# Plain fp32 scores for the first head pair alone, idle matmuls at the start, loads held back until the first q has landed, and a longer time for loads in the plan

## The chip, the cores and the metric

The kernel runs on one core of one Trainium2 chip. The metric is the device time of one execution in microseconds; the kernel before was run three times and its median stands. One execution was also profiled, and all rows below are from that one. The engines are PE (TensorE), ACT (ScalarE), DVE (VectorE), POOL (GpSimd) and SP, which issues the transfers (DMA).

## The reference

Attention with rotary positions over 8 batches, 8 heads, 576 positions and 64 columns a head, and then a gated MLP over each batch:

```python
    q_rot, k_rot = (rotate(q), rotate(k))
    scores = scale * np.matmul(q_rot, k_rot.transpose(0, 1, 3, 2))
    scores = scores - np.max(scores, axis=-1, keepdims=True)
    attn = np.exp(scores)
    attn = attn / (np.sum(attn, axis=-1, keepdims=True) + 1e-09)
    return np.matmul(attn, v).astype(np.float32)
...
    h = np.maximum(x @ w_in, 0.0)
    u, v = (h[..., :d_ff // 2], h[..., d_ff // 2:])
    v_n = (v - mu) / np.sqrt(var + 1e-06)
    v_s = np.einsum('ts,bsd->btd', w_spatial, v_n) + b_spatial[None, :, None]
    gated = u * v_s
    return (gated @ w_out).astype(np.float32)
```

The MLP has d_model 512 and d_ff 1024; w_spatial is 576 x 576. Inputs are float32 but for w_in and w_out, which are 64-bit floats.

## The kernel before

The work is cut into 32 head pairs (8 batches of four pairs), numbered i, and one MLP for each batch. Every step of the work is an entry made with `op` (or `either`, where two engines may take it): an engine, a planned cost in ns, a priority key, a function that emits the instructions, the tokens it reads and writes, and the buffers it opens. `Program.run` (L137) then plays all entries through a planned clock: whenever an engine is free it takes the ready entry with the smallest key whose buffers are free, and emits it. So the plan fixes the order of each engine's instructions, and on the chip each engine follows its own order and waits by semaphores. A step counts as done at its cost plus a fixed time of its engine (`LATENCY`, L31; 1700 ns for DMA, 200 for PE). A step with `port=True` is not started while the other of DVE and POOL holds such a step. All transfers go out through SP, in the plan's order. Keys run at about 20 a pair.

A pair's scores are nine row tiles of 128 queries: (head, t) for t = 0 to 3 and one mixed tile t = 4 that holds the last 64 queries of both heads. Each tile goes PE (`scores`, L521), DVE maximum (L557), ACT exponent (L559), through two PSUM buffers (`sc`). There are two ways to make a tile. Pairs below `WHOLE` (L53) use `prepare_whole` (L444): q and k are turned and the fp32 product is taken plainly over the 64 columns of a head (`mm_whole`, L538; rows at L546). All others use `prepare`: q and k are turned in two staging buffers (`stage`), ACT rounds each to fp32r (L416, L427), POOL or DVE takes the rest (`lo_q`, `lo_k`), and ten transfers (L438) stack rounded parts and rests over 128 partitions in `qs`, `ks` and `qz`, of which there is one each; `lk` has one buffer too. Its products are fp32r (`mm`, L528; rows at L536). Pairs below `PLAIN` = 4 take the values with plain transposes (L635) and products (L673) in `values_plain`, the others in `values` (L576, L600).

The start is written out in `prepare_whole` for i = 0: k and the tables come in halves, then q; DVE turns k, sums it, and then turns q in two parts, columns 0 to 191 for tile t = 0 and the rest for the others (L469 to L472). `setup` (L289) makes the identity and the fills on POOL. `decode` (L317) turns the 64-bit weights into rounded float32 parts, twelve times, with keys 30 to 132 (`DEC_V`, `DEC_U`, `DEC_O`); `spatial` (L356) and `spatial_tail` do the like for w_spatial. The MLP's products are at L744, L767, L785 and L800.

Of the kernel before, what the change touches and what calls it, by code (L numbers as in the profile page):

```python
# [16 lines left out]
P = 128  # L17
S = 576
# [11 lines left out]
PE, ACT, DVE, POOL, DMA = "pe", "act", "dve", "pool", "dma"  # L30
LATENCY = {PE: 200, ACT: 142, DVE: 118, POOL: 95, DMA: 1700}  # L31
TO_PE = 105
SLOTS = {
    "stage": 2, "lk": 1, "vraw": 2, "vs": 2, "e2": 4, "e1": 2, "eh": 7, "rb": 1, "x32": 1, "xg": 7, "m": 4,
    "small": 3, "nmx": 3, "rt": 2, "sc": 2, "pv": 1, "pm": 3,
# [14 lines left out]

PLAIN = 4

WHOLE = 3  # L53
Q0 = 3 * TW
CHUNKS2 = [
    ([(0, 0), (1, 0), (0, 1), (1, 1), (0, 2), (1, 2)], [(0, P, 0, 0, 384)]),
# [42 lines left out]
class Op:  # L99
    def __init__(self, costs, key, f, new, port):  # L100
        self.costs, self.key, self.f, self.new, self.port = costs, key, f, new, port
        self.eng = None
        self.waits, self.after, self.bufs = 0, [], []


class Program:
# [5 lines left out]
    def op(self, eng, ns, key, f, r=(), w=(), new=(), port=False):  # L112
        return self.either({eng: ns}, key, lambda e: f(), r, w, new, port)
# [23 lines left out]
    def run(self, make):  # L137
# [29 lines left out]
        while events:  # L167
# [23 lines left out]
            for e in LATENCY:  # L191
                if busy[e]:
                    continue
                passed, chosen = [], None
                while ready[e] and not chosen:
                    item = heapq.heappop(ready[e])
                    if item[2].eng:
                        continue
                    other = {DVE: POOL, POOL: DVE}.get(e)
                    if item[2].port and other and held[other]:  # L200
                        passed.append(item)
                    elif place(item[2].new):
                        chosen = item[2]
                    else:
                        passed.append(item)
                for item in passed:
                    heapq.heappush(ready[e], item)
                if chosen:
                    for b in chosen.new:
                        b.tile = make(b)  # L210
                    chosen.eng = e
                    chosen.f(e)
                    left -= 1
                    busy[e], held[e] = True, chosen.port
                    heapq.heappush(events, (now + chosen.costs[e], n, "free", e))
                    heapq.heappush(events, (now + chosen.costs[e] + LATENCY[e], n + 1, "done", chosen))
                    n += 2
        assert not left, "instructions wait for each other"
        return now
# [3 lines left out]
def tile_attention_gated_mlp(  # L223
# [81 lines left out]
    def load(dst, src):  # L305
        nc.sync.dma_start(out=dst, in_=src)  # L306
# [10 lines left out]
    def decode(key, where, at, src):  # L317
# [38 lines left out]

    def spatial(key, j):
        st = Buf("xg", [P, 2, S], F32, f"ws{j}")
        op(DMA, 1700, key - 8, lambda: load(st.tile, w_spT[j * P:(j + 2) * P, :].rearrange("(c p) t -> p c t", p=P)), w=[st], new=[st])
# [21 lines left out]
    def prepare(i):  # L381
# [24 lines left out]
            pair_op(S, key - K_SUM, f, first=eng, r=[(st[j], 1)], w=[(st[j], 0)])  # L406

        for j in range(2):
            op(DMA, 1640, key - K_LOAD, lambda j=j: load(st[j][:, :2 * S], qk[b, hp, j].rearrange("p c n -> p (c n)")), w=[(st[j], 0), (st[j], 1)], new=[st[j]])
        op(DMA, 910, key - K_LOAD + 1, lambda: load(vr.tile, v[b, hp]), w=[vr], new=[vr])  # L410
        for j, eng, part in ROPE0 if b == 0 else ROPE:
            if part is None:
                rope_sum(j, eng)
# [30 lines left out]
    def prepare_whole(i, b, hp, key):  # L444
# [7 lines left out]
        def turn(st, part, cols):  # L452
            return st[:, S * part:S * part + S][:, cols]
# [5 lines left out]
        if i == 0:  # L459
            for part in range(2):  # L460
                cols = slice(S * part, S * part + S)
                op(DMA, 820, -70 + part, lambda part=part, cols=cols: load(k[:, cols], qk[b, hp, 1, :, part]), w=[(k, part)], new=[] if part else [k])
                op(DMA, 820, -70 + part, lambda part=part, cols=cols: load(tabs[:, cols], tab[:, part]), w=[("tabs", part)])
            op(DMA, 1640, -68, lambda: load(q.tile, qk[b, hp, 0].rearrange("p c n -> p (c n)")), w=[q], new=[q])
            op(ACT, 1053, -50, lambda: nc.scalar.activation(tabq, tabs, AF.Copy, scale=0.125), r=[("tabs", 0), ("tabs", 1)], w=["tabq", "tabs"])
            for part in range(2):
                op(DVE, 680, -60, lambda part=part: nc.vector.tensor_tensor(out=turn(k, part, slice(0, S)), in0=turn(k, part, slice(0, S)), in1=turn(tabs, part, slice(0, S)), op=ALU.mult), r=[("tabs", part)], w=[(k, part)], port=True)
            op(DVE, 830, -59, lambda: sum_k(nc.vector), r=[(k, 0), (k, 1)], w=[kf], new=[kf], port=True)
            for n, (c0, c1) in enumerate(((0, Q0), (Q0, S))):  # L469
                cols = slice(c0, c1)  # L470
                op(DVE, dve_ns(2 * (c1 - c0)), -58 + 2 * n, lambda cols=cols: nc.vector.scalar_tensor_tensor(out=c2(q.tile)[:, :, cols], in0=c2(q.tile)[:, :, cols], scalar=0.125, in1=c2(tabs)[:, :, cols], op0=ALU.mult, op1=ALU.mult), r=[q, ("tabs", 0), ("tabs", 1)], w=[(q, n)], port=True)
                op(DVE, dve_ns(c1 - c0), -57 + 2 * n, lambda cols=cols: nc.vector.tensor_tensor(out=turn(q, 0, cols), in0=turn(q, 0, cols), in1=turn(q, 1, cols), op=ALU.add), w=[(q, n)], port=True)  # L472
        else:
            for j, st in enumerate((q, k)):
                t = ("tabq", "tabs")[j]
                op(DMA, 1640, key - K_LOAD, lambda j=j, st=st: load(st.tile, qk[b, hp, j].rearrange("p c n -> p (c n)")), w=[(st, 0), (st, 1)], new=[st])
# [4 lines left out]
        op(DMA, 910, key - K_LOAD + 1, lambda: load(vr.tile, v[b, hp]), w=[vr], new=[vr])  # L481


    def attention(i):
# [361 lines left out]

    pairs = [(b, hp) for b in range(B) for hp in range(NP)]
    prepped, xs, chain = [], [], []
    op(POOL, 800, -26, setup, w=["ident", "bias", ("sums", 0, 0), ("sums", 1, 0), ("qz", 0), ("qz", 1), ("qs", 0, 0), ("qs", 1, 0)])
# [84 lines left out]
```

## Time and profile before

| | us |
|---|---|
| median of 3 runs | 981.48 |
| lowest and highest | 977.74 and 984.55 |
| the profiled execution | 979.22 |
| its span, first to last instruction | 977.4 |

In the rows, times are microseconds from the span's start unless marked ns. A row of the timeline is: start, duration, engine, source line, operation, what it writes and reads, how often, and in brackets the idle time of the engine before it with what ended it. PE is matmul, PEld the loading of its weights, SPq the issue of a transfer. Ends of matmuls are modelled by the profiler.

### The profile page before, as it was taken

Reading aid. Unit: us, or ns where it says so; the run is one execution under the profiler, and the core shown is the slowest. Engines: PE = TensorE matmul, PEld = TensorE weight load, DVE = VectorE, ACT = ScalarE, POOL = GpSimd, SP = SyncE. Lnnn points to the kernel's source line nnn. Section 1 sums busy time; section 2 is a strip of 40 time slices with the busy share of each in tenths; the row PEclk is TensorE's granted clock in tenths of the full one; section 3 lists DMA queues with packets and bytes.
Section 4 is the critical chain, followed back from the end, with each engine's and each line's share of the span. In section 5 each row is a group of like instructions: output and inputs, shape, how many; then the busy total and the mean of one; then the engine's idle time right before and its main releaser. Section 6 shows DMA issues by size and latency. Waiting matters only on the chain.

```text
span 977.4 us, 19421 instructions
## 1 busy us (share of the span) xinstructions
PE 942.1 (96%) x6618; PEld 853.3 (87%) x6618; DVE 672.1 (69%) x1486; ACT 733.9 (75%) x1827; POOL 571.6 (58%) x500
## 2 busy tenths in 40 slices
PE   4999999999999999999999999999999999999998
PEld 2455689998899989999899988999889998999998
DVE  6999898765866677675776658676686756767331
ACT  3778788777987779776897768877798677976452
POOL 5852445556757657774756766666576765672121
PEclk9999999999999999999999999999999999999999
DMA  7761733454344553345444444445524455330101
GB/s 295 221 197 52 209 100 108 130 128 140 99 139 117 153 150 101 111 120 165 120 130 108 118 151 126 118 128 149 139 76 132 126 156 145 98 93 17 62 2 49
DMA packets 54581, 121.56 MB, mean 124 GB/s; under 512 B 12881, under 2 KB 12881, under 8 KB 54482
## 3 DMA queue, kind: packets, MB, share of 16 engines
q1 hardware_dynamic: 54482, 120.32, 43.1%
q8 instruction: 53, 0.87, 0.4%
q14 instruction: 46, 0.38, 0.1%
HBM read 66.03 MB, written 9.58 MB: 77 GB/s over the span
## 4 chain that ended last, share of the span: by engine, by line
PE 59%; ACT 14%; DMA 9%; DVE 8%; POOL 4%; issue 3%; SPq 2%; DVEq 0%; ACTq 0%; POOLq 0%
PE pc L785 12%; PE sc L536 9%; PE pv L600 8%; PE tp L576 8%; PE pd L800 7%; PE pa L744 4%; PE pb L767 4%; ACT e L559 4%; DMA qs<-st 3%; POOL st L401 2%; ACT eh L587 2%; DVE nmx L557 2%; SPq L306 2%; PE sc L546 2%; ACT vv L827 2%
## 5 line engine op out<-in xcount | busy, mean ns | idle before, releaser
L587 ACT ACTIVATE eh<-tp 128x384 fp32r<-128x384 f32 (+1 forms) x504 | 217.5, 433 | 85.6 <-PE tp L576 69.5
L312 DVE TENSOR_TENSOR el<-tp,eh 128x384 fp32r<-128x384 f32 x336 | 185.9, 554 | 105.1 <-ACT eh L587 92.6
L559 ACT ACTIVATE e<-sc,nmx 128x576 f32<-128x576 f32 x288 | 213.0, 741 | 39.1 <-DVE nmx L557 36.7
L557 DVE TENSOR_REDUCE nmx<-sc 128x1 f32<-128x576 f32 x288 | 215.2, 749 | 31.8 <-PE sc L536 23.4
L576 PE MATMUL tp<-ident,e 128*128 128x128 f32 (+1 forms) x1176 | 197.1, 273 | 11.6 <-ACT ob L803 7.7
L576 PEld LDWEIGHTS tp<-ident,e 128*128 128x128 f32 (+1 forms) x1176 | 144.5, 138 | 30.4 <-ACT ob L803 9.1
L401 POOL TENSOR_TENSOR st<-st,tabq 128x576 f32<-128x576 f32 x55 | 77.7, 1427 | 135.9 <-DMA st<-in_qk_dram 131.0
L600 PE MATMUL pv<-eh,vs 128*128 128x384 f32 (+1 forms) x560 | 154.0, 316 | 0.1
L785 PE MATMUL pc<-wsp,vn 128*128 128x288 f32 x768 | 143.3, 304 | 0.8 <-DVE u L843 0.5
L767 PE MATMUL pb<-x,wi 128*128 128x288 f32 x768 | 142.3, 306 | 0.7 <-ACT u L770 0.7
L800 PE MATMUL pd<-g,wo 128*128 128x288 f32 x768 | 140.8, 304 | 0.0
L744 PE MATMUL pa<-wi,x 128*128 128x512 f32 x448 | 133.0, 407 | 0.0
L536 PE MATMUL sc<-ks,qs 128*128 128x288 f32 x580 | 123.2, 302 | 0.0
L785 PEld LDWEIGHTS pc<-wsp,vn 128*128 128x128 f32 x768 | 115.0, 189 | 3.4 <-DVE u L843 0.9
L710 POOL TENSOR_TENSOR x<-x,rb 128x576 f32<-128x576 f32 x31 | 44.3, 1429 | 123.7 <-DVE x L615 93.4
L767 PEld LDWEIGHTS pb<-x,wi 128*128 128x128 f32 x768 | 112.3, 189 | 4.4 <-PE pb L767 1.4
L800 PEld LDWEIGHTS pd<-g,wo 128*128 128x128 f32 x768 | 113.5, 189 | 2.6
L600 PE MATMUL pv<-el,vs 128*64 128x384 f32 (+1 forms) x448 | 113.7, 295 | 0.0
L536 PE MATMUL sc<-lk,qz 128*128 128x288 f32 x522 | 111.9, 295 | 0.0
L600 PEld LDWEIGHTS pv<-eh,vs 128*128 128x128 f32 x560 | 97.7, 188 | 5.8 <-DVE x L615 1.6
L312 DVE TENSOR_TENSOR eh<-tp,eh 64x256 fp32r<-64x256 f32 (+1 forms) x168 | 59.8, 356 | 61.4 <-ACT eh L587 52.3
L536 PEld LDWEIGHTS sc<-ks,qs 128*128 128x128 f32 x580 | 93.1, 189 | 6.3 <-ACT e L559 0.8
(180 smaller groups left out, 1559.2 us busy)
## 6 DMA issues: line engine op xcount, KB each, us to landing
st<-in_qk_dram SPq DMA_DIRECT2D x63, 576.0 KB
ks<-st SPq DMA_DIRECT2D x116, 160.0 KB
qs<-st SPq DMA_DIRECT2D x116, 144.0 KB
vr<-in_v_dram SPq DMA_DIRECT2D x32, 320.0 KB
out_dram<-ob SPq DMA_DIRECT2D x32, 288.0 KB
qz<-st SPq DMA_DIRECT2D x58, 144.0 KB
ws<-in_w_spT_dram SPq DMA_DIRECT2D x2, 576.0 KB
st<-in_qk_dram SPq DMA_DIRECT2D x2, 288.0 KB
```

The lines of the kernel that those rows point to most:

```text
L312: eng.tensor_tensor(out=lo, in0=src, in1=hi.bitcast(F32), op=ALU.subtract)
L401: f = lambda e: e.tensor_tensor(out=st[j][:, cols], in0=st[j][:, cols], in1=(tabs if j else tabq)[:, cols], op=ALU.mult)
L536: nc.tensor.matmul(pt[:, c * 512:c * 512 + HALF], lhsT=lhsT, rhs=rhs[:, k0 + c * HALF:k0 + (c + 1) * HALF], start=(n == 0), stop=(n == len ...
L557: op(DVE, 665, key + K_MAX, lambda: nc.vector.tensor_reduce(out=nmx.tile, in_=tops(), op=ALU.max, axis=AX.XY, negate=True), r=[pt], w=[nmx ...
L559: op(ACT, 730, key + K_EXP, lambda: nc.scalar.activation(e[:, e0:e0 + S].rearrange("p (c n) -> p c n", c=2), tops(), AF.Exp, bias=nmx.tile ...
L576: nc.tensor.transpose(out=tp[:e.shape[1], m * P:m * P + P], in_=e, identity=ident)
L587: nc.scalar.activation(h, p, AF.Copy)
L600: nc.tensor.matmul(pv[0:rows, c1:c2], lhsT=vs[:, kt, h, vp, :], rhs=part[:, c1:c2], start=(kt == 0 and n == 0 and c1 == 0), stop=last)
L744: nc.tensor.matmul(pm.tile, lhsT=lhsT, rhs=win[1, d][:, j, :], start=(d == 0 and n == 0), stop=(d == 3 and n == len(todo) - 1))
L767: nc.tensor.matmul(pm[:, :HALF], lhsT=win[0, d][:, i, f * P:(f + 1) * P], rhs=x[d][:, at:at + HALF], start=(d == 0 and n == 0), stop=(d == ...
L785: nc.tensor.matmul(pm[:, :HALF], lhsT=lhsT, rhs=rhs, start=(t == 0 and n == 0), stop=(t == 4 and n == 1))
L800: nc.tensor.matmul(pm[:, :HALF], lhsT=wout[d,][:, i, m * P:(m + 1) * P], rhs=gs[d][:, at:at + HALF], start=(d == 0 and n == 0), stop=(d == ...
```

## The change

`WHOLE` goes from 3 to 1: pairs 1 and 2 are prepared and scored like pair 3. Twenty matmuls of the identity with itself are entered on PE with keys from 10000 on, so that the plan takes one only where PE has nothing else that is ready; each opens the one `pv` buffer, whose contents nobody reads. The identity is made in a step of its own with key -80, ahead of the fills. A token "first" is written by the load of the first q, and the loads of all other pairs, of v, of w_in and w_out and of two of the three parts of w_spatial read it: none is issued before q has landed. DVE's steps at the start are merged: the second half of k with its sums, and each part of q with its sum. From pair 4 on the loads of q and k count 1500 ns longer in the plan (`LATE`), which emits nothing.

```diff
+LATE = 1500
-WHOLE = 3
+WHOLE = 1
...
-        self.eng = None
+        self.eng, self.late = None, 0
...
-                    heapq.heappush(events, (now + chosen.costs[e] + LATENCY[e], n + 1, "done", chosen))
+                    heapq.heappush(events, (now + chosen.costs[e] + LATENCY[e] + chosen.late, n + 1, "done", chosen))
...
     def setup():
-        make_identity(nc, ident)
...
-        op(DMA, 1500, key - 8, fetch, w=[t0, t1])
+        op(DMA, 1500, key - 8, fetch, r=["first"], w=[t0, t1])
...
         for j in range(2):
-            op(DMA, 1640, key - K_LOAD, lambda j=j: load(...), w=[(st[j], 0), (st[j], 1)], new=[st[j]])
+            o = op(DMA, 1640, key - K_LOAD, lambda j=j: load(...), r=["first"], w=[(st[j], 0), (st[j], 1)], new=[st[j]])
+            o.late = LATE if i >= 4 else 0
...
-            op(DMA, 1640, -68, lambda: load(q.tile, ...), w=[q], new=[q])
+            op(DMA, 1640, -68, lambda: load(q.tile, ...), w=[q, "first"], new=[q])
...
+            def turn_k(part):
+                nc.vector.tensor_tensor(out=turn(k, part, slice(0, S)), in0=turn(k, part, slice(0, S)), in1=turn(tabs, part, slice(0, S)), op=ALU.mult)
+                if part:
+                    sum_k(nc.vector)
+
+            def turn_q(cols):
+                both = c2(q.tile)[:, :, cols]
+                nc.vector.scalar_tensor_tensor(out=both, in0=both, scalar=0.125, in1=c2(tabs)[:, :, cols], op0=ALU.mult, op1=ALU.mult)
+                nc.vector.tensor_tensor(out=turn(q, 0, cols), in0=turn(q, 0, cols), in1=turn(q, 1, cols), op=ALU.add)
+
+            op(DVE, 680, -60, lambda: turn_k(0), r=[("tabs", 0)], w=[(k, 0)], port=True)
+            op(DVE, 1600, -60, lambda: turn_k(1), r=[("tabs", 1)], w=[(k, 0), (k, 1), kf], new=[kf], port=True)
             for n, (c0, c1) in enumerate(((0, Q0), (Q0, S))):
+                op(DVE, dve_ns(2 * (c1 - c0)) + dve_ns(c1 - c0), -58 + 2 * n, lambda c0=c0, c1=c1: turn_q(slice(c0, c1)), r=[q, ("tabs", 0), ("tabs", 1)], w=[(q, n)], port=True)
...
-    op(POOL, 800, -26, setup, w=["ident", "bias", ...])
+    op(POOL, 800, -80, lambda: make_identity(nc, ident), w=["ident"])
+    op(POOL, 800, -26, setup, w=["bias", ...])
+    for n in range(20):
+        idle = Buf("pv", None, None, f"idle{n}")
+        op(PE, 480, 10000 + n, lambda idle=idle: nc.tensor.matmul(idle[:, :P], lhsT=ident, rhs=ident, start=True, stop=True), r=["ident"], w=[idle], new=[idle])
```

## Rows read from the trace of the kernel before

**Rows 1.** The page: busy time by engine, and the granted clock in 40 slices.

```profile
PE 942.1 (96%) x6618; PEld 853.3 (87%) x6618; DVE 672.1 (69%) x1486; ACT 733.9 (75%) x1827; POOL 571.6 (58%) x500
...
PEclk9999999999999999999999999999999999999999
```

**Rows 2.** Stretches: busy us (and count) by engine, granted clock, DMA share, GB/s.

```profile
10.00:20.00 10.00, 7.20 (x22) 4.70 (x23) 6.96 (x11) 3.18 (x8) 7.88 (x5) 1.00 0.69 279
...
20.00:30.00 10.00, 8.39 (x28) 4.41 (x26) 8.67 (x14) 6.29 (x14) 4.30 (x4) 1.00 0.92 330
...
30.00:100.00 70.00, 65.84 (x382) 36.33 (x382) 65.19 (x112) 57.06 (x137) 37.90 (x35) 1.00 0.47 143
...
110.00:190.00 80.00, 77.93 (x542) 68.72 (x541) 66.97 (x146) 64.80 (x163) 38.96 (x31) 1.00 0.46 122
```

**Rows 3.** Timeline of the start, on POOL, DVE and PE.

```profile
1.02 0.29 POOL masks.py:199 TENSOR_SCALAR_AFFINE_SELECT ident<-ident 128x128 f32<-128x128 f32 x1
...
6.59 0.76 DVE L467 TENSOR_TENSOR st<-st,tabs 128x576 f32<-128x576 f32 x1 [1.24 <-DMA tabs<-in_tab_dram]
...
8.30 1.43 DVE L471 SCALAR_TENSOR_TENSOR st<-st,tabs 128x384 f32<-128x384 f32 x2
...
8.77 0.95 DVE L471 SCALAR_TENSOR_TENSOR st<-st,tabs 128x768 f32<-128x768 f32 x1
...
9.64 0.82 DVE L472 TENSOR_TENSOR st<-st 128x192 f32<-128x192 f32 x2
...
10.05 2.30 PE L546 MATMUL sc<-kf,st 64*128 64x288 f32 x8 [10.05 <-DVE st L472]
```

**Rows 4.** L546's matmuls in 10 to 31, then 38 to 76 us: ns min/median/max.

```profile
L546 PE MATMUL sc<-kf,st x40: 684/684/846, 10.0 to 29.0; 64*128 64x288 f32 x32, 64*64 64x288 f32 x8
...
L546 PE MATMUL sc<-kf,st x72: 402/403/507, 38.0 to 75.5; 64*128 64x288 f32 x56, 64*64 64x288 f32 x16
```

**Rows 5.** Timeline of PE: the same forms at different times.

```profile
25.18 0.90 PE L635 MATMUL tp_0a<-ident,e 128*128 128x128 f32 x3
...
27.49 2.19 PE L546 MATMUL sc<-kf,st 64*64 64x288 f32 x8
...
31.73 1.31 PE L546 MATMUL sc<-kf,st 64*128 64x288 f32 x8
...
49.53 0.55 PE L635 MATMUL tp_0a<-ident,e 128*128 128x128 f32 x3
...
50.48 1.19 PE L546 MATMUL sc<-kf,st 64*64 64x288 f32 x8
```

**Rows 6.** The chain of work that ended last: start, us, engine, tile, line.

```profile
38.12 1.17 PE sc L546 x4
...
88.39 0.52 PE sc L536 x4
```

**Rows 7.** Timeline of SPq and PE, pair 3's values and pair 4's stacking.

```profile
95.00 0.48 SPq L306 DMA_DIRECT2D qs<-st  x1
...
96.53 0.55 PE L635 MATMUL tp_1a<-ident,e 128*128 128x128 f32 x3 [0.75 <-ACT et_0b L642]
...
99.15 0.55 PE L635 MATMUL tp_2a<-ident,e 128*128 128x128 f32 x3 [0.65 <-DVE et_1b L644]
...
101.09 0.50 PE L536 MATMUL sc<-ks,qs 128*128 128x288 f32 x2
```

**Rows 8.** Preparing: the page's POOL group, a step of the chain, POOL's timeline.

```profile
L401 POOL TENSOR_TENSOR st<-st,tabq 128x576 f32<-128x576 f32 x55 | 77.7, 1427 | 135.9 <-DMA st<-in_qk_dram 131.0
...
2.12 4.37 DMA tabs<-in_tab_dram
...
29.83 1.44 POOL L456 TENSOR_TENSOR kf<-st 128x576 f32<-128x576 f32 x1 [1.56 <-PE sc L546]
```

**Rows 9.** Waits after 110 us: us in total, times, longest.

```profile
PE tp L576 <- ACT ob L803: 7.7, 6, 1.5
...
POOL st L401 <- DMA st<-in_qk_dram: 131.0, 24, 7.9
```

More of the change, by code (lines that the diff above doesn't have):

```diff
@@ L358, in spatial @@
         st = Buf("xg", [P, 2, S], F32, f"ws{j}")
-        op(DMA, 1700, key - 8, lambda: load(st.tile, w_spT[j * P:(j + 2) * P, :].rearrange("(c p) t -> p c t", p=P)), w=[st], new=[st])
+        op(DMA, 1700, key - 8, lambda: load(st.tile, w_spT[j * P:(j + 2) * P, :].rearrange("(c p) t -> p c t", p=P)), r=["first"], w=[st], new=[st])
         for c in range(2):
@@ L408, in prepare @@
         for j in range(2):
-            op(DMA, 1640, key - K_LOAD, lambda j=j: load(st[j][:, :2 * S], qk[b, hp, j].rearrange("p c n -> p (c n)")), w=[(st[j], 0), (st[j], 1)], new=[st[j]])
-        op(DMA, 910, key - K_LOAD + 1, lambda: load(vr.tile, v[b, hp]), w=[vr], new=[vr])
+            o = op(DMA, 1640, key - K_LOAD, lambda j=j: load(st[j][:, :2 * S], qk[b, hp, j].rearrange("p c n -> p (c n)")), r=["first"], w=[(st[j], 0), (st[j], 1)], new=[st[j]])
+            o.late = LATE if i >= 4 else 0
+        op(DMA, 910, key - K_LOAD + 1, lambda: load(vr.tile, v[b, hp]), r=["first"], w=[vr], new=[vr])
         for j, eng, part in ROPE0 if b == 0 else ROPE:
@@ L463, in prepare_whole @@
                 op(DMA, 820, -70 + part, lambda part=part, cols=cols: load(tabs[:, cols], tab[:, part]), w=[("tabs", part)])
-            op(DMA, 1640, -68, lambda: load(q.tile, qk[b, hp, 0].rearrange("p c n -> p (c n)")), w=[q], new=[q])
+            op(DMA, 1640, -68, lambda: load(q.tile, qk[b, hp, 0].rearrange("p c n -> p (c n)")), w=[q, "first"], new=[q])
             op(ACT, 1053, -50, lambda: nc.scalar.activation(tabq, tabs, AF.Copy, scale=0.125), r=[("tabs", 0), ("tabs", 1)], w=["tabq", "tabs"])
-            for part in range(2):
-                op(DVE, 680, -60, lambda part=part: nc.vector.tensor_tensor(out=turn(k, part, slice(0, S)), in0=turn(k, part, slice(0, S)), in1=turn(tabs, part, slice(0, S)), op=ALU.mult), r=[("tabs", part)], w=[(k, part)], port=True)
@@ L468, in prepare_whole @@
-            op(DVE, 830, -59, lambda: sum_k(nc.vector), r=[(k, 0), (k, 1)], w=[kf], new=[kf], port=True)
+            def turn_k(part):
[6 more added lines that the diff above has]
+                nc.vector.tensor_tensor(out=turn(q, 0, cols), in0=turn(q, 0, cols), in1=turn(q, 1, cols), op=ALU.add)
@@ L469, in prepare_whole @@
+            op(DVE, 680, -60, lambda: turn_k(0), r=[("tabs", 0)], w=[(k, 0)], port=True)
+            op(DVE, 1600, -60, lambda: turn_k(1), r=[("tabs", 1)], w=[(k, 0), (k, 1), kf], new=[kf], port=True)
             for n, (c0, c1) in enumerate(((0, Q0), (Q0, S))):
-                cols = slice(c0, c1)
-                op(DVE, dve_ns(2 * (c1 - c0)), -58 + 2 * n, lambda cols=cols: nc.vector.scalar_tensor_tensor(out=c2(q.tile)[:, :, cols], in0=c2(q.tile)[:, :, cols], scalar=0.125, in1=c2(tabs)[:, :, cols], op0=ALU.mult, op1=ALU.mult), r=[q, ("tabs", 0), ("tabs", 1)], w=[(q, n)], port=True)
@@ L472, in prepare_whole @@
-                op(DVE, dve_ns(c1 - c0), -57 + 2 * n, lambda cols=cols: nc.vector.tensor_tensor(out=turn(q, 0, cols), in0=turn(q, 0, cols), in1=turn(q, 1, cols), op=ALU.add), w=[(q, n)], port=True)
+                op(DVE, dve_ns(2 * (c1 - c0)) + dve_ns(c1 - c0), -58 + 2 * n, lambda c0=c0, c1=c1: turn_q(slice(c0, c1)), r=[q, ("tabs", 0), ("tabs", 1)], w=[(q, n)], port=True)
         else:
@@ L475, in prepare_whole @@
                 t = ("tabq", "tabs")[j]
-                op(DMA, 1640, key - K_LOAD, lambda j=j, st=st: load(st.tile, qk[b, hp, j].rearrange("p c n -> p (c n)")), w=[(st, 0), (st, 1)], new=[st])
+                op(DMA, 1640, key - K_LOAD, lambda j=j, st=st: load(st.tile, qk[b, hp, j].rearrange("p c n -> p (c n)")), r=["first"], w=[(st, 0), (st, 1)], new=[st])
                 for part in range(2):
@@ L480, in prepare_whole @@
             pair_op(S + TW, key - K_SUM, sum_k, pieces=2, r=[(k, 0), (k, 1)], w=[kf], new=[kf])
-        op(DMA, 910, key - K_LOAD + 1, lambda: load(vr.tile, v[b, hp]), w=[vr], new=[vr])
+        op(DMA, 910, key - K_LOAD + 1, lambda: load(vr.tile, v[b, hp]), r=["first"], w=[vr], new=[vr])
     def attention(i):
@@ L848, in tile_attention_gated_mlp @@
     prepped, xs, chain = [], [], []
-    op(POOL, 800, -26, setup, w=["ident", "bias", ("sums", 0, 0), ("sums", 1, 0), ("qz", 0), ("qz", 1), ("qs", 0, 0), ("qs", 1, 0)])
+    op(POOL, 800, -80, lambda: make_identity(nc, ident), w=["ident"])
+    op(POOL, 800, -26, setup, w=["bias", ("sums", 0, 0), ("sums", 1, 0), ("qz", 0), ("qz", 1), ("qs", 0, 0), ("qs", 1, 0)])
+    for n in range(20):
+        idle = Buf("pv", None, None, f"idle{n}")
+        op(PE, 480, 10000 + n, lambda idle=idle: nc.tensor.matmul(idle[:, :P], lhsT=ident, rhs=ident, start=True, stop=True), r=["ident"], w=[idle], new=[idle])
     prepare(0)
```

## Prediction

> **What bounds the kernel now.** I read the page first: TensorE is busy 942 of 977 us [rows 1], so the end moves only if its work shrinks or its gaps do. The stretches come next [rows 2]. From 110 us on TensorE is full (77.9 of 80 us) and no edit there can do more than close the small gaps. Between 10 and 30 us it is busy for 15.6 of 20 us, and in 30 to 100 it has 65.8 of 70 while VectorE has 65.2. So what the change can win lies ahead of 100 us.
>
> The timeline of the start [rows 3] shows TensorE doing nothing for 10.05 us. The last table half lands just before 6.59, VectorE works through k and then q, and the first scores follow the last VectorE instruction. Of that chain the 0.95 us product over the larger part of q (the x1 row at 8.77, columns 192 on, for row tiles 1 to 4) stands ahead of both sums, and the first tile doesn't need it.
>
> The third thing is hidden by the page. The granted clock reads full in every slice [rows 1], but the same fp32 score matmul takes 684 ns at the median in 10 to 31 us and 403 ns in 38 to 76 [rows 4]. The transposes do the same: three take 0.90 us at 25 us and 0.55 at 49 [rows 5]. The durations say that pair 0's scores run at the lower of TensorE's two levels (1.2 GHz against 2.4), though TensorE was busy three quarters of that time. Only the dense work from 30 us on is quick.
>
> **Scores of pairs 1 and 2.** Before, a pair costs one double tile (two heads side by side, 1.31 us at 31.73), six single tiles of 1.17 and the mixed tile t=4 of 1.19 [rows 5, 6]: 1.31 + 7.02 + 1.19 = 9.5 us. Split into rounded parts, as pair 3 already is, a tile takes 0.52 us [rows 6]; t=4 has six matmuls for four, so 0.78 as an estimate: 8 x 0.52 + 0.78 = 4.9. That is 4.6 us a pair, **9.1 us** for two, on the engine that sets the end.
>
> What it adds beside the path: for each pair two roundings on ScalarE, two subtractions on POOL or VectorE, and ten stacking transfers through SP. POOL has the room (37.9 of 70 us busy in 30 to 100 [rows 2]), so I count the subtractions at nothing; on VectorE the cover is thin. VectorE's 65.2 of 70 us is partly twelve weight decodes that run early because they can. The eight for wi0 and wo have keys above 64, later than much of the scores, and may slide behind 100 us, where VectorE is busy for 67 of 80 us. If the decodes had to finish as early as now, VectorE and not TensorE would set that stretch.
>
> What it adds to the path: qs, ks, qz and lk have one buffer each. Pair 3 could be stacked early because pairs 1 and 2 did not use them; now pair 2 is stacked only behind pair 1's last scores, and pair 3 behind pair 2's. The case before for pair 4 [rows 7]: stacking begins at 95.00 and the first score comes at 101.09, 6.1 us; TensorE fills them with values and loses 0.75 + 0.65 = 1.4 us. Two more such turnovers cost **2.8 us** that way, and 12.2 with nothing to fill them; nothing if values cover all. I take 2.8, because the same values (fourteen groups of transposes a pair at 0.55 and their products) stand ready.
>
> The staging buffer has two slots, one pair. So there is a ring: stacking frees it, the next load goes out, POOL turns and splits, stacking again. By the rows that is 6.1 us + 4.4 (a load's issue to landing, the tables' half) + eight POOL steps of 1.43 [rows 8] = 21.9 us a pair. The pairs now follow each other, from 31.73 to 101.09, at 23.1 us each [rows 5, 7]; less the 4.6 it would be 18.5. If POOL must do it alone, the ring is 3.4 us a pair too slow, 6.8 for two. VectorE's 0.76 us [rows 3] for the same step shortens it, which is why I stay at 2.8.
>
> **The start.** The merged VectorE steps put the first 192 columns of q (product and sum) ahead of the 0.95 us product: **0.9 us** earlier, so the first score near 9.15 (bounds: nothing, if q lands late; 0.9). The gate holds every other load until q has landed, near 8 us, since q is used at 8.30 without a wait. Queued behind that wait on SP are pair 0's and pair 1's loads and all raw weights, in that order. SP had issued them right behind q; now pair 1's data come some 2 us later, as an estimate: the transfers stand still from q's landing until the next issue's data flow, about half of the 4.4 us from an issue to its landing [rows 8]. Pair 1's last k sum ran only at 29.83 and its first score at 31.73 [rows 5, 8], so I count the gate at nothing; without the cover of pair 0's values it costs those 2 us. The five loads of the start meet no others, which can only help.
>
> **The idle matmuls.** The identity is ready at 1.31 [rows 3], and now first on POOL. In the plan they start at 1.0 us and follow each 0.68 us; the first score is planned at about 7.6, so some ten go ahead of it and ten into the gaps between score tiles. A transpose of that size takes 0.30 us at the lower level; an fp32 product has two records, so I estimate 0.6 us, ten in 6 us, done by 7.5, inside the 10.05 us of nothing. Those in the gaps find waits of a microsecond or more (TensorE is busy 15.6 of 20 us), two at a time; I count nothing, at most 3 us for ten at 0.3.
>
> What they bring: at the full level each of the four double tiles needs 1.31 for the 2.30 us of the first [rows 3, 5], and each is followed by maximum, exponent and the next tile's start, so the difference falls on the path: 4 x 0.99 = 4.0. The mixed tile goes from 2.19 to 1.19 (1.0), three groups of transposes from 0.90 to 0.55 (1.05) [rows 5]. Sum **6.0 us** (bounds: 0 if the clock does not hold; 6.0).
>
> The Trainium skill, page "TensorE: Matmul & The Clock Gate", Part 1, says the low clock is the default and activity lifts it; the durations at either side of 31 us agree, and the granted clock of the page does not show it. By that rule alone the gain would be the 6.0 us. The same page, "HAM oscillation", says that an idle stretch of TensorE lowers the clock again; by that the ten early matmuls would be wasted if the stretch up to 9.15 us is idle long enough, and the gain would be 0. No run here shows which.
>
> **Loads counted longer.** This changes only the plan from pair 4 on: turning steps are placed 1.5 us later. POOL waits 131 us for these loads, TensorE's largest wait there is 7.7 us in six places [rows 9]. At best these 7.7 go; at worst a later preparation adds as much. I take 0.
>
> **Sum.** -9.1 - 6.0 - 0.9 + 2.8 = -13.2 us. The profiled execution took 979.2 (span 977.4 and 1.8 around it), so 966.0; the median of the runs is 2.3 above it, 981.5, so **968.3 us**.
>
> **Rivals.**
> *The clock does not hold.* For it: in 10 to 30 us TensorE was busy 15.6 of 20 us and stayed slow, and after the idle matmuls there are some 2 us of nothing. Against it: ten more fill the gaps, and from 80 us on it has gaps of 0.75 us at full speed. Time: 968.3 + 6.0 = 974.3.
> *The ring of staging bounds pairs 1 to 3.* For it: VectorE's 65.2 of 70 us leaves the turning to POOL; then 6.8 for the 2.8 and, since POOL also has the spatial weights to split, a few us more: 973 to 979.
> *Slower.* The same ring, if SP's order is wrong: the stacks of a pair stand behind raw weight loads whose buffers or gate come late, and every pair waits. Pair 1 would begin near 25 us, three pairs follow to pair 4's first score at 101.09: up to 25.4 us each the change gains, from there it loses; at 28.7 us a pair it is 1% slower, 991. Against: nothing in the rows takes 7 us beyond the 21.9.
> *More than forecast.* The longer count takes most of the 7.7: 961.
>
> **How the numbers follow.** Forecast 0.50 (own range 963 to 974), more 0.07, clock 0.18, ring 0.17, slower 0.08. The range leaves out the slower case, half of the best one and the edges: 958 to 982. One per cent, 9.8 us, is about what a measurement here can tell from no change. Below 971.7 lie the best case and most of the forecast, and a little of the two middle ones: 0.55 faster; 0.37 within; 0.08 slower.
>
> **What would show it.** First score near 9.1; L546 medians at 403 ns from the start on (684: the clock rival); fp32r scores of pair 1 near 25 us; pair 4's first score near 88 instead of 101, with TensorE's waits between pairs under 2 us each (if 5 and up, waiting on stacks: the ring); from there on the same busy share to the end. I am wrong if pair 4's first score comes early and the end doesn't, since then VectorE's decodes or the new plan took it back.

## The result, and the profile after

The kernel after takes 969.25 us (median of 4 runs, 967.38 to 971.53), beside 983.01 us for the kernel before in the same comparison (4 runs, 977.74 to 986.14): ratio 0.9862, 95% interval 0.9825 to 0.9899. It is 13.8 us faster. The forecast was 968.3. The time fits; most of the working behind it does not, as the profile shows already. The profiled execution took 971.53 us, its span is 969.8. It lies only 7.7 us below the profiled execution of the kernel before (979.22); the other 6.1 of the 13.8 us stand in the medians and in no trace.

First the page after (busy time; the granted clock in 40 slices), to be read against [rows 1]:

```profile
PE 948.5 (98%) x6654; PEld 863.4 (89%) x6654; DVE 670.6 (69%) x1479; ACT 738.1 (76%) x1837; POOL 580.0 (60%) x507
...
PEclk9999999999999999999999999999999999999999
```

TensorE is busier than before, 948.5 for 942.1 us, in a shorter span: the cheaper scores take work off it, and the idle matmuls put more on (some 16 us by their rows). Then the two long stretches of [rows 2], after (columns as there):

```profile
30.00:100.00 70.00, 64.33 (x415) 40.59 (x413) 65.25 (x112) 57.48 (x142) 43.99 (x39) 1.00 0.75 221
110.00:190.00 80.00, 77.01 (x536) 68.79 (x537) 66.43 (x148) 66.78 (x169) 37.98 (x32) 1.00 0.46 118
```

VectorE has 65.25 of 70 us as before; what grew is POOL (37.90 to 43.99) and the transfers (0.47 to 0.75 of the DMA engines' time). Now the start after, on PE, DVE and SP, the answer to [rows 3]:

```profile
1.37 8.47 PE L862 MATMUL idle<-ident 128*128 128x128 f32 x20 [1.37 <-POOL ident masks.py:199]
10.59 2.30 PE L555 MATMUL sc<-kf,st 64*128 64x288 f32 x8 [0.74 <-DVE st L476]
...
7.56 0.76 DVE L469 TENSOR_TENSOR st<-st,tabs 128x576 f32<-128x576 f32 x1 [2.23 <-DMA tabs<-in_tab_dram]
...
9.59 0.56 DVE L475 SCALAR_TENSOR_TENSOR st<-st,tabs 128x384 f32<-128x384 f32 x1 [0.34 <-DMA st<-in_qk_dram]
...
3.07 1.19 SPq L306 DMA_DIRECT2D wst<-in_w_spT_dram  x2
...
4.83 0.38 SPq L306 DMA_DIRECT2D vr<-in_v_dram  x1
5.26 1.26 SPq L306 DMA_DIRECT2D st<-in_qk_dram  x2
```

Three steps of the prediction fall here. The first score runs at 10.59, not 9.1. It takes the same 2.30 us as before, so the idle matmuls had not lifted the clock by then. And SP issues the small `wst` loads at 3.07, then `vr` and pair 1's `st` at 4.83 and 5.26, long before q is there (VectorE waits for q until 9.59): the token "first" orders the plan, and on the chip nothing waits for it. The line of the plain scores after (ns min/median/max, first and last start) says the same of the clock as the upper row of [rows 4]:

```profile
L555 PE MATMUL sc<-kf,st x32: 684/684/847, 10.6 to 28.9; 64*128 64x288 f32 x32
```

Pair 1's first score comes at 35.77 us and pair 4's at 105.23, where 25 and 88 were forecast and 31.73 and 101.09 stood before [rows 5, 7]:

```profile
35.77 0.51 PE L545 MATMUL sc<-ks,qs 128*128 128x288 f32 x2
...
105.23 0.43 PE L545 MATMUL sc<-ks,qs 128*128 128x288 f32 x2
```

LATE begins at pair 4 and moves that score itself; without LATE (the run late0 below) it comes at 102.33, still behind the 101.09. So not one microsecond was won in the stretch that was to bring all of it. What changed is in TensorE's waits behind 110 us (us in total, times, longest):

```profile
PE tp L585 <- DVE eh L312: 2.1, 2, 1.2
PE sc L545 <- ACT e L568: 1.4, 2, 0.9
PE pc L794 <- DVE el L312: 0.7, 1, 0.7
```

The 7.7 us for ScalarE's evacuation `ob` [rows 9] are gone. To place the gain I cut every kernel's span at two events: the first MLP product `pa` of batch 1 and that of batch 7. Between them lies the same work in all kernels. These are windows of one stretch each, first before, then after:

```profile
230.70:918.10 687.40, 678.00 (x4917) 641.25 (x4917) 473.06 (x1086) 542.63 (x1366) 431.14 (x367) 1.00 0.44 121
```

```profile
229.00:910.50 681.50, 677.60 (x4918) 641.39 (x4917) 473.55 (x1086) 543.37 (x1365) 432.48 (x368) 1.00 0.46 122
```

The six batches take 687.4 us before and 681.5 after. TensorE is busy the same 678 us in both; its idle time fell from 9.4 to 3.9. The start, up to batch 1, brings 1.7 (230.7 to 229.0), the end behind batch 7's first `pa` nothing. The only part of the change that reaches this stretch is LATE, the one that was priced at nothing.

### The profile page after: what moved, and what is told of

The parts are those of the page before. It is cut to its first block, busy times and chain, and to the rows that moved or that the text cites. A ratio compares the mean times of both kernels' runs of the same rounds, so it can differ in the third digit from the quotient of the medians.

```text
span 969.8 us, 19571 instructions
## 1 busy us (share of the span) xinstructions
PE 948.5 (98%) x6654; PEld 863.4 (89%) x6654; DVE 670.6 (69%) x1479; ACT 738.1 (76%) x1837; POOL 580.0 (60%) x507
## 3 DMA queue, kind: packets, MB, share of 16 engines
HBM read 66.03 MB, written 9.58 MB: 78 GB/s over the span
## 4 chain that ended last, share of the span: by engine, by line
PE 69%; ACT 10%; DVE 10%; DMA 6%; issue 2%; POOL 1%; SPq 1%; DVEq 0%; ACTq 0%; POOLq 0%
PE pc L794 12%; PE sc L545 11%; PE pv L609 11%; PE tp L585 10%; PE pd L809 10%; PE pb L776 8%; PE pa L753 4%; ACT e L568 3%; DVE nmx L566 3%; DMA st<-in_qk_dram 2%; ACT eh L596 2%; ACT vv L836 2%; DVE el L312 1%; DMA qz<-st 1%; DMA qs<-st 1%
## 5 line engine op out<-in xcount | busy, mean ns | idle before, releaser
L401 POOL TENSOR_TENSOR st<-st,tabq 128x576 f32<-128x576 f32 x59 | 84.0, 1440 | 147.5 <-DMA st<-in_qk_dram 132.4
L545 PE MATMUL sc<-ks,qs 128*128 128x288 f32 x620 | 132.0, 302 | 3.8 <-ACT e L568 1.8
L545 PE MATMUL sc<-lk,qz 128*128 128x288 f32 x558 | 119.3, 295 | 0.0
L545 PEld LDWEIGHTS sc<-ks,qs 128*128 128x128 f32 x620 | 99.8, 188 | 14.5 <-ACT e L568 6.4
```

Source lines behind the costliest of these rows:

```text
L401: f = lambda e: e.tensor_tensor(out=st[j][:, cols], in0=st[j][:, cols], in1=(tabs if j else tabq)[:, cols], op=ALU.mult)
L545: nc.tensor.matmul(pt[:, c * 512:c * 512 + HALF], lhsT=lhsT, rhs=rhs[:, k0 + c * HALF:k0 + (c + 1) * HALF], start=(n == 0), stop=(n == len ...
```

## The experiments

All of them stand beside runs of the kernel before on the same chip (its medians there: 981.6 to 982.6 us).

### LATE by itself, and everything but LATE

In the kernel after, and in the kernel before:

```diff
-LATE = 1500          # the kernel after -> late0
+LATE = 0
...
+LATE = 1500          # the kernel before -> only_late
+            o.late = LATE if i >= 4 else 0
```

> The changed kernel with LATE = 0, all else kept. Theory A (the longer count of loads in the plan earns the gain, since batch 0 ends where it did before and the lead grows only from batch 1 on): the gain goes, 979 to 984 us, and the spacing from one batch's first L753 product to the next is that of before, about 115.5 us. Theory B (the cheaper scores of pairs 1 and 2 and the start earn it): 968 to 971 us, spacing about 113.5 us.

> The kernel before with the longer count of loads alone. Theory A: 969 to 975 us, batches 113.5 us apart. Theory B: 981 to 985 us, no change, batches 115.5 us apart. Rival C (any new order of the plan moves the later batches by some us, the count is not special): anything between, with spacings that differ from batch to batch.

Measured: without LATE 990.16 us, ratio 1.0094 (1.0059 to 1.0129), so the other four edits together make the kernel slower, and by more than theory A's 979 to 984. LATE alone 968.92, ratio 0.9859 (0.9833 to 0.9885), the whole gain of the change. The same windows, LATE alone and then without LATE:

```profile
228.80:907.90 679.10, 677.19 (x4917) 641.80 (x4916) 473.37 (x1086) 543.03 (x1365) 431.93 (x368) 1.00 0.45 123
```

```profile
240.90:928.80 687.90, 677.98 (x4918) 640.97 (x4917) 472.89 (x1086) 542.25 (x1366) 430.92 (x367) 1.00 0.45 121
```

With LATE the six batches take 679.1 and 681.5 us (TensorE idle 1.9 and 3.9), without it 687.4 and 687.9 (idle 9.4 and 9.9). Of the 10.3 us between the spans of the kernel before and of LATE alone (977.4, 967.1), 8.3 lie between these two events and 1.9 ahead of them. The medians differ by 13.7; the profiled execution of the kernel before (979.2) lies 3.4 under the median beside it, so 3.4 us of the gain are in no trace.

What the other four edits cost without LATE lies ahead of batch 1, which begins 10.2 us later than in the kernel before (240.9 to 230.7). From 90 to 240 us TensorE waits there for exponents (4.8 us in five places), and its clock falls twice (last section). So in the kernel after LATE is worth 20.9 us and not 13.7, and the larger part of it comes ahead of batch 1 (240.9 to 229.0; behind it 687.9 to 681.5).

What LATE changes on the chip can be followed at one place. The kernel before, timeline of SP, POOL, ACT and PE around 220 us:

```profile
214.65 2.81 SPq L306 DMA_DIRECT2D st<-in_qk_dram  x2
...
220.58 2.81 POOL L401 TENSOR_TENSOR st<-st,tabq 128x576 f32<-128x576 f32 x2 [7.88 <-DMA st<-in_qk_dram]
...
224.75 1.40 POOL L405 TENSOR_TENSOR st<-st 128x576 f32<-128x576 f32 x1
...
226.18 0.68 ACT L309 ACTIVATE st<-st 128x576 fp32r<-128x576 f32 x1 [2.36 <-DMA rb<-rt7d]
226.77 0.39 ACT L803 ACTIVATE ob<-pd 128x288 f32<-128x288 f32 x1
...
225.07 0.64 PE L800 MATMUL pd<-g,wo 128*128 128x288 f32 x3
227.22 0.55 PE L576 MATMUL tp<-ident,e 128*128 128x128 f32 x3 [1.50 <-ACT ob L803]
```

The load of q and k is issued at 214.65, and POOL, which has waited 7.88 us for it, turns at 220.58 and sums at 224.75 to 226.15. ScalarE has the rounding of that sum (L309) at the head of its queue and starts it at 226.18, as the sum ends; the row's bracket names another transfer, but POOL's sum is the input that comes last. Behind the rounding, in the same queue, stands the evacuation `ob`, whose input has been ready since 225.7 or so (TensorE's L800 before it ends there); it runs at 226.77, and TensorE, which needs a PSUM buffer (its memory for results), has lost 1.50 us. The plan had placed the rounding ahead of the evacuation; that it did so because it took the load for done too early follows from LATE, which changes nothing else and turns the two round. The same place with LATE alone (ACT, then PE):

```profile
224.62 0.40 ACT L805 ACTIVATE ob<-pd 128x288 f32<-128x288 f32 x1
...
225.89 0.69 ACT L310 ACTIVATE st<-st 128x576 fp32r<-128x576 f32 x1
...
225.41 0.49 PE L578 MATMUL tp<-ident,e 128*128 128x128 f32 x3
```

The load comes no sooner (POOL still waits 7.44 us here), but an evacuation now stands ahead of the rounding and PE's transposes wait for nothing. Six waits of TensorE for `ob` make up the 7.7 us of [rows 9]; this is the longest. Its waits for ScalarE's `u` (2.1 us in three places, same queue) are gone with them. The kernel after repeats it: 6.6 us for `ob` in six places without LATE (late0), none with it. The other five places were not followed row by row.

### LATE twice as long

```diff
-LATE = 1500          # only_late -> late3000
+LATE = 3000
```

> The kernel before with LATE alone, at 3000 ns in place of 1500. Theory L (the 1500 ns already put the q and k roundings behind the evacuations: after 110 us only 2.7 of the 11.8 us of TensorE's waits are left, none of them behind ACT's ob): nothing more is to be had, 967 to 970 us. Rival S (the count is still short: POOL waits up to 8.4 us for a load in the kernel with 1500): the waits that are left shrink too, below 967. Rival T (preparations planned still later now hold up the next pair's scores): above 972, with waits of TensorE for stacks or for lk.

Measured: 984.02 us, ratio 1.0019 (1.0000 to 1.0037). Theories L and S are both wrong and T has the size, but not the sign that it named: one wait for stacks of 0.6 us is all there is. The rows (the window between the two `pa`; waits of TensorE in it; the window of 80 to 100 us):

```profile
234.70:921.10 686.40, 680.67 (x4918) 641.45 (x4918) 476.18 (x1086) 545.92 (x1366) 434.71 (x369) 1.00 0.44 122
```

```profile
PE tp L578 <- ACT ob L805: 3.2, 5, 0.7
PE sc L538 <- DMA ks<-st: 0.6, 1, 0.6
```

```profile
80.00:100.00 20.00, 18.44 (x104) 11.12 (x105) 16.36 (x29) 13.32 (x32) 1.10 (x3) 0.86 0.05 16
```

Batch 1 begins 5.9 us later than with 1500 (234.7 to 228.8), where POOL now stands nearly idle from 80 to 100 us (1.10 us busy) and TensorE's granted clock is 0.86; and the six batches take 7.3 us longer, with five waits for `ob` back and TensorE's busy time up by 3.5. So LATE is no correction that helps the more the truer it is. It shifts an order, and 1500 gives a good one, which is luck: 0, 1500 and 3000 ns give 982.6, 968.9 and 984.0 us. Which evacuations the 3000 puts behind what was not followed row by row.

### The scores of pairs 1 and 2, the gate and the idle matmuls

```diff
-WHOLE = 1            # the kernel after -> whole3
+WHOLE = 3
...
-    for n in range(20):          # the kernel after -> noidle
+    for n in range(0):
...
-r=["first"],                     # the kernel after, all six -> nogate
```

nogate_noidle is both of the latter: the kernel before with LATE, WHOLE = 1, the identity made first and the merged VectorE steps.

> The changed kernel with WHOLE = 3: pairs 1 and 2 in plain fp32 again. Prediction as written: 9.1 - 2.8 = 6.3 us slower than the changed kernel, 975 to 976 us. Theory A (that stretch is set by VectorE or by the staging, not by TensorE's products): within 2 us of the changed kernel, 967 to 971 us, or a little faster.

> The changed kernel without the twenty idle matmuls. Prediction as written: 6.0 us slower, 975 us. The trace of the changed kernel shows L555 at 684 ns and more up to 29 us, so the clock rival says: within 1 us, 968 to 970 us, or up to 2 us faster, since the matmuls in the gaps then delay no scores.

> The changed kernel without the token of the first load; the idle matmuls stay. The trace of the changed kernel shows that the token orders the plan alone: SP sends the spatial tail at 3.07 and v at 4.83, before q is there. Theory G (the only effect is that the tail slips ahead, and the tables land at 7.5 instead of 6.5): first score 1 us earlier, 967 to 969 us. Rival (the plan's order is better with it): 970 us and more.

> The kernel before with the longer count, the cheaper scores of pairs 1 and 2 and the merged steps, without token and idle matmuls. Prediction as written: 6.3 us below the 968.9 of the count alone, 962 to 964 us. Theory D (VectorE or the staging sets the stretch to 110 us): 967 to 971 us, with the first L753 product near 105 us as in the others.

Measured, with the ratio to before: whole3 975.35 us, 0.9941 (0.9917 to 0.9965); noidle 970.28, 0.9888 (0.9857 to 0.9918); nogate 972.10, 0.9901 (0.9863 to 0.9939); nogate_noidle 968.76, 0.9853 (0.9823 to 0.9883). So whole3 does what the prediction says and nogate_noidle does not; noidle agrees with the clock rival, nogate with the rival that the plan's order is better with the gate. Together with only_late at 968.92 they make a square:

| | scores plain in three pairs | in the first alone |
|---|---|---|
| LATE, without gate and idle matmuls | 968.92 (only_late) | 968.76 (nogate_noidle) |
| LATE, with gate and idle matmuls | 975.35 (whole3) | 969.25 (after) |

The upper left cell also lacks the merged steps. Below, the cheaper scores bring 6.1 us, as much as the forecast's 9.1 less 2.8. Above they bring nothing. So they are worth something only where gate and idle matmuls have first cost something, and the best corner is no better with them than without. Where the latter cost is seen in pair 1's first score: 35.77 us with gate and idle matmuls, and with the gate alone (noidle)

```profile
30.80 0.50 PE L545 MATMUL sc<-ks,qs 128*128 128x288 f32 x2
```

with neither it is 29.70 (nogate_noidle). At the low clock the idle matmuls between pair 0's tiles hold up the tiles (the third begins at 19.82 us, in noidle at 17.67). For the corner above, the windows and waits of TensorE show where the 9.1 go. First only_late, then nogate_noidle, 30 to 100 and 100 to 171 us:

```profile
30.00:100.00 70.00, 65.90 (x382) 36.21 (x378) 64.71 (x111) 56.28 (x133) 37.25 (x34) 1.00 0.47 143
100.00:171.00 71.00, 69.84 (x472) 58.76 (x473) 57.84 (x131) 58.41 (x149) 34.94 (x29) 1.00 0.49 140
```

```profile
30.00:100.00 70.00, 62.86 (x405) 38.98 (x403) 64.84 (x113) 57.77 (x140) 48.01 (x42) 1.00 0.74 217
100.00:171.00 71.00, 65.31 (x432) 56.17 (x431) 58.62 (x127) 57.15 (x142) 33.97 (x27) 0.98 0.46 130
```

TensorE is busy 7.6 us less over the 141 us (135.7 and 128.2), and behind it nogate_noidle isn't ahead (batch 1 begins at 228.8 and at 230.4). The time became waits, and that late: at batch 0's first `pa` the cheaper scores still lead by 4.5 us (only_late, then nogate_noidle):

```profile
105.66 0.96 PE L746 MATMUL pa<-wi,x 128*128 128x512 f32 x3
```

```profile
101.21 0.96 PE L753 MATMUL pa<-wi,x 128*128 128x512 f32 x3
```

From 100 us on TensorE then idles 5.7 of 71 us, where only_late idles 1.2. TensorE's waits from 30 to 171 us, the largest of nogate_noidle:

```profile
PE sc L545 <- ACT e L568: 2.7, 4, 1.4
PE tp_1a L644 <- ACT et_0b L651: 1.6, 2, 1.0
PE pb L776 <- DVE sm L828: 1.4, 1, 1.4
PE tp_2a L644 <- DVE et_1b L653: 1.1, 1, 1.1
```

They come to 12.3 us in all there, 4.8 in only_late. None is large, and they stand behind ScalarE and VectorE in turn: exponents, copies of transposed values, the MLP's statistics. In this stretch TensorE doesn't set the pace alone.

### VectorE's decodes cut

To see whether VectorE sets it: in eight of the twelve weight decodes three of VectorE's six steps are left out (about 15 us; these weights go without their low words, signs and exponents), in only_late (late_cut) and in nogate_noidle (cheap_cut).

```diff
+        if not (where is win and at[0] == 1):
+            op(DVE, 640, key, bits(0xFFFFF, 0x100000, ALU.bitwise_and, ALU.bitwise_or), r=[t1], w=[pt])
+            op(ACT, 480, key, high, r=[pt, t0], w=[t0, t1, (n, "hi")])
+            op(DVE, 640, key, lambda: rest_lo(...), r=[pt, (n, "hi")], w=[n])
+            return
```

> The kernel before with the longer count, and three of the six VectorE steps left out in the eight decodes of the first half of w_in and of w_out (those weights come out wrong): 24 steps, some 15 us of VectorE's work. Theory D (VectorE sets the stretch to 171 us): below the 968.9 of the count alone, 962 to 966 us, by then limited by TensorE's plain scores. Theory R (staging and turnovers set it): 967 to 969 us.

> The same cut in the kernel with the longer count, the cheaper scores and the merged steps (968.8 us without the cut, so that the cheaper scores brought 0.2 us there). Theory D: the scores' 6.3 us of the prediction appear, 5 to 7 us below late_cut. Theory R: within 2 us of late_cut, since the turnovers between pairs 1 to 4 stay.

Measured: late_cut 968.99 us, ratio 0.9871 (0.9845 to 0.9896), no gain over only_late. cheap_cut 965.46, 0.9824 (0.9801 to 0.9848), 3.5 under late_cut and between the numbers of the two theories. So with plain scores in three pairs VectorE is not the limit, and with cheap scores it takes back about half of the 6.3 us that were forecast. The rest stays open: in cheap_cut TensorE is still busy for only 61.68 of the 70 us from 30 on, and its largest wait there is for exponents (3.7 us in six places). The cut doesn't tell VectorE's time from a second thing that it shortens: a decode holds one of three PSUM buffers (`pm`) over all its steps, and TensorE's transposes take theirs from the same three. How much that can cost is seen in the run `hot` below.

### The clock of the first 30 us

Idle matmuls of another kind: 24 of 512 columns back to back, before the first score, in the kernel before with LATE (late_hot) and in place of the twenty in the kernel after (hot). Then, in the former, 20 such and pairs of them entered into the waits between pair 0's tiles (late_fill).

```diff
+        for n in range(24):
+            nc.tensor.matmul(heat.tile, lhsT=vn[:, 0, 0, :P], rhs=vn[:, 0, 0, :], start=(n == 0), stop=(n == 23))
...
+    for n in range(14):          # late_fill, after a first block of 20
+        op(PE, 300, 10000 + n, run_fill, r=[("vn", 0, 0)], w=[heat])
```

> The kernel before with the longer count of loads, and 24 dense matmuls of 512 columns ahead of the first score, in one step and one buffer, so that none waits for another. Theory W (TensorE's level is raised by dense work and holds through pair 0's scores): L548 near 403 ns from the first score on, 4 to 6 us off the 968.9 of the kernel with the count alone, 963 to 965 us. Theory F (the waits between pair 0's scores bring it down again): L548 back at 684 ns after the first tiles, 967 to 970 us.

> The changed kernel with the same 24 dense matmuls in place of the twenty idle ones. Theory W: 963 to 965 us, against 970.3 without any and 969.3 with the twenty. Theory F: 968 to 972 us. Rival (pair 1's operands are then what is late): the first scores are quick, but pair 1's first score stays near 30 us and the time near 968.

> The kernel before with the longer count, 20 dense matmuls ahead of the first score and pairs of dense matmuls in the waits between pair 0's score tiles, all in one buffer and without waits of their own. If the waits are what brings TensorE's level down (theory F of the run before), it now holds: L548 near 403 ns in 10 to 25 us, pair 0's tiles 3 us apart and not 4, the 6.0 us of the prediction less the 1 already in the run before: 962 to 964 us. If something behind it takes the lead (pair 1's operands, VectorE): quick tiles but 966 to 969 us.

Measured: late_hot 968.13 us, 0.9849 (0.9819 to 0.9879); hot 977.08, 0.9936 (0.9913 to 0.9959); late_fill 968.11, 0.9870 (0.9839 to 0.9902). The timeline of late_hot on PE, and its windows:

```profile
10.11 1.25 PE L548 MATMUL sc<-kf,st 64*128 64x288 f32 x8 [1.36 <-DVE st L474]
13.11 3.00 PE L548 MATMUL sc<-kf,st 64*128 64x288 f32 x8 [1.76 <-ACT e L561]
```

```profile
9.00:12.00 3.00, 1.25 (x8) 0.71 (x8) 2.88 (x5) 0.00 (x0) 1.43 (x1) 0.96 1.02 413
12.00:30.00 18.00, 13.51 (x41) 7.98 (x41) 15.60 (x22) 9.43 (x22) 11.53 (x9) 0.50 0.81 303
```

The dense block lifts the clock: the first double tile takes 1.25 us for 2.30. It falls again at about 11.75 us, since the 9 to 12 us have 0.96 and what follows 0.50: behind 1.36 us of idle ahead of that tile and the first 0.4 us of the wait for its exponents. The second tile takes 3.00, the granted clock is 0.50 from 12 to 30 us, and the rest is as before. The Trainium skill, page "TensorE: Matmul & The Clock Gate", section "HAM oscillation", says that waits between groups of matmuls bring the low clock back; this trace agrees, with 1.36 and 0.4 us of idle about one tile of 1.25. With the gaps filled (late_fill) the clock does hold. The plain scores' line of 10 to 30 us, then ACT and PE behind it:

```profile
L548 PE MATMUL sc<-kf,st x45: 402/403/507, 11.2 to 30.0; 64*128 64x288 f32 x37, 64*64 64x288 f32 x8
```

```profile
33.29 1.25 ACT L310 ACTIVATE wsp<-ws 128x576 fp32r<-128x576 f32 x2 [2.67 <-DMA ws<-in_w_spT_dram]
34.45 0.47 ACT L644 ACTIVATE et_2b<-tp_2b 128x384 f32<-128x384 f32 x1
...
34.97 0.86 PE L675 MATMUL pv<-et_2b,vr 128*64 128x384 f32 x2 [1.86 <-ACT et_2b L644]
```

403 ns from the first score on, pair 0's transposes 2.6 us earlier (tp_1a at 27.89 for 30.48) and no gain at the end that can be told from only_late. Right behind, ScalarE waits 2.67 us at the head of its queue for a part of w_spatial, which only_late rounds at 33.10 without a wait; TensorE's next operand is queued behind that, and TensorE waits. The clock falls (0.63 from 36 to 45 us), and the first `pa` comes at 108.5 us where only_late has 105.7. It is the mechanism of 220 us once more: work came earlier, the load did not. But this execution took 971.43 us. Three of the five runs have a mean clock of 1.000, so none of this fall, and took 966.98 to 968.11, at most some 2 us under only_late; what keeps those from the 6.0 us is in no trace.

The twenty idle matmuls of the change can lift the clock as well. In nogate, which has them all and ten of them ahead of the first score as the kernel after has, the scores are quick from the second tile on, and pair 1 begins near where the prediction put it:

```profile
L555 PE MATMUL sc<-kf,st x40: 402/403/847, 9.8 to 25.5; 64*128 64x288 f32 x32, 64*64 64x288 f32 x8
```

```profile
26.33 0.54 PE L545 MATMUL sc<-ks,qs 128*128 128x288 f32 x2
```

TensorE had no wait ahead of nogate's first score and 0.18 us ahead of the second; in the kernel after it had 0.74 and 0.25. Whether that, the gate or the moment at which the tables land makes the difference can't be told from one execution of each. At the end it brings nothing (972.10); the clock is at 0.50 again from 45 to 53 and from 95 to 102 us.

`hot` is slower than every theory had it and 7.8 us slower than the kernel after, and its trace says where. Batch 1 begins at 238.6 us for 229.0, and before that stands one wait:

```profile
101.01 0.90 PE L644 MATMUL tp_0a<-ident,e 128*128 128x128 f32 x3 [6.17 <-DVE wo L312]
```

Three decodes of w_out are under way on VectorE at that time (it is busy for all of 95 to 100 us), each holds one of the three `pm` buffers, and the transpose gets its buffer when the first is done. TensorE's clock is at 0.50 from 95 to 107 us.

## Why the prediction was right or wrong

**Right in the time, wrong in where it comes from.** That the sum fits is luck. The forecast of -13.2 us was made of -9.1, -6.0, -0.9 and +2.8. LATE alone gives -13.7, and what those four terms stand for gives, with it, nothing that can be told from zero (968.92 to 969.25), and costs 7.6 us without it (982.6 to 990.2). The prediction named the sign by which it would be wrong as pair 4's first score early and the end not; what came is the reverse, the score late (105.23) and the end early.

**Loads counted longer: the step that failed.** The text gave it 0 with 7.7 us either way, and "more than forecast" 7 in 100. Before it the text had read TensorE as full from 110 us on, by 77.9 of 80 us, and looked for the gain ahead of 100 us; the 11.8 us of its waits behind 110 us are where the gain came from. [rows 9] had the right row and the term was mis-sized: a plan in which POOL waits 131 us for loads is a plan whose clock runs ahead, and everything that POOL feeds through an in-order queue is then early in that queue. With LATE alone TensorE's idle time between batch 1 and batch 7 fell by 7.5 us, so the upper bound was about what happened there, and the value taken, 0, was the wrong one to take; with the rest of that stretch, what lies ahead of batch 1 and what no trace holds the gain is 13.7. The other side shows at 3000 ns, which gives back all of it. "Emits nothing" was read as "changes little"; a plan's duration reorders every queue behind it.

**The clock.** The term of -6.0 is wrong. In the kernel after the clock had no rise to hold: the idle matmuls had not lifted it by the first score. Ten of them (two records each) go ahead of it, as planned, and take 8.47 us, 0.85 each for the estimated 0.6. Each opens the same buffer, and its weights are loaded only when the one before it has ended, 0.35 of the 0.85 us; TensorE's own rows have it busy for 7.95 of the 8.47. The profile's view of that line, up to 30 us, has the loading of weights (PEld) wait for it (us, times):

```profile
  PEld idle L862: 4.2, 12
```

These waits alone don't keep the clock low, since nogate has them too, and there it rose. Back to back and wider, idle matmuls lift it before the first score (late_hot). The ten in the gaps were counted at nothing, at most 3 us; in the kernel after they come to 0.8 us each, and pair 1's first score is 5.0 us later than without them (30.80, 35.77), 1.0 of which its first tile is late by already (9.58, 10.59). In the total they gain or cost nothing that shows (970.28 without them, 969.25 with), though the profiled run without them has 10 us at half clock (0.50 from 87 to 97 us) that the kernel after doesn't have. Even a clock that holds brings nothing to the end (late_fill, nogate): the bound of 6.0 took each tile to lie on the path, and in late_fill's trace a load does.

**The start.** Read from the landing of the second table half, the merged steps work as priced: from VectorE's first step on it to the first score it is 3.46 us before (6.59, 10.05) and 2.61 in nogate_noidle (7.24, 9.85), 0.85 less. In the kernel after it is 3.03, since q comes 0.34 us too late. But that step itself starts anywhere between 6.46 (noidle) and 8.48 us (whole3) in the traces of these runs, though SP's first five issues are the same in all, and that is more than the 0.9.

**The gate.** It was said to hold the other loads until 8 us. It holds none of them on the chip, it only changes their order, and lets the three small `wst` and bias loads slip ahead of v and pair 1's q and k. By itself it moves pair 1 little, as was counted: its first score is at 30.80 with the gate and 29.70 without, when there are no idle matmuls. In nogate, which drops it, the time is not better (972.10; its interval and that of after overlap).

**Scores and turnovers.** Cost per tile and the two turnovers of the sum were sound: after shows a wait of 1.27 us for pair 2's stacks and 0.71 for another transfer, 2.0 us for the 2.8. But the sum took TensorE as the engine that sets the end of 30 to 100 us because it had 65.8 of 70 us; with VectorE at 65.2 beside it that was a tie. TensorE's 9.1 us became 7.6 us less busy time and as much waiting. The text had seen this ("VectorE and not TensorE would set that stretch") and trusted that the decodes could slide; the cut decodes show that they, by VectorE's time or by the buffers that they hold, account for about half.

## What to carry to other kernels

When engines follow queues that a plan has ordered, compare the plan's durations with the trace before costing anything else: a load that the plan takes for done too soon puts its consumer at the head of a queue, and what waits behind it (here a PSUM evacuation) stops the engine that sets the time. Such a correction is tried at several values, because it selects an order and doesn't scale; 1500 ns won 14 us here and 3000 won nothing. When a trace explains why an edit won nothing, see first whether its execution is like the others. And a total that comes out right says nothing of its terms: undo each edit alone, and do each alone.

## What the runs showed of the hardware

The granted clock of the trace shows a low stretch in one case and not in another. It reads 1.00 up to 30 us in the kernels before and after, while fp32 matmuls of one form take 684 ns, and 403 once the clock is up [rows 4]. In late_hot the same 684 ns from 12 to 30 us stand beside 0.50: there the clock had risen before. So up to the first rise the durations tell the clock, and the granted clock doesn't.

TensorE's clock also falls later, in the thin stretch between 45 and 125 us, in some kernels and there in some executions. In whole3 (profiled at 982.81; the seven of its runs that have a mean clock of 0.998 or more lie between 972.25 and 976.22):

```profile
45.50:62.50 17.00, 17.00 (x61) 8.87 (x59) 8.74 (x14) 8.87 (x22) 6.28 (x6) 0.51 0.41 102
```

TensorE is busy all of these 17 us at half its clock, and the other engines are about half idle, so a fall here costs time. In hot it is 12 us at 95 to 107, in late0 two falls of 3 and 6 us between 110 and 123. The mean clock of each run shows how often: 0.982 to 0.984 in all six of hot, 0.989 to 0.996 in all of noidle and nogate, 0.999 to 1.000 in all four of the kernel after. That cheaper scores bring the falls, because TensorE has less to do there, isn't shown: whole3 and late3000, with plain scores in three pairs, have them too.
